# Sliding-window attention and gated convolution on one core: a 32x32-tile convolution for 12 of 56 pairs, and a new order

## The chip, the core and the metric

The kernel runs on one core of a Trainium2 chip. The metric is the device time of one execution in microseconds (us). The profile is one further execution, recorded by the hardware profiler; its times are us, unless ns is written. The engines are PE (matrix multiply; PEld is its weight load), DVE (vector), ACT (scalar, activations), POOL (gpsimd) and SP, which issues the DMA transfers. Every engine works through its own instructions strictly in program order and meets the others at semaphores.

## The reference

```python
scores = 1/sqrt(64) * q @ k.T                     # q, k, v: 8 batches, 8 heads, 576, 64
scores = where(|i - j| <= 32, scores, -1e9)
attn   = softmax(scores);  x = attn @ v           # x: 8, 576, 512
h      = relu(x @ w_in)                           # w_in: 512, 1024
conv   = sum over k of conv_w[k] * h shifted by k - 1   # 3 taps along the sequence, one weight a channel
out    = (h * sigmoid(conv)) @ w_out              # w_out: 1024, 512; out is float32
```

Inputs and output are float32; the kernel multiplies in bf16 and accumulates in float32.

## The kernel before

**An order written out.** The program is a list of some 860 words, ORDER (L30), each a step with its arguments. A loop at L742 calls the step's function. The class Pinned (L183) keeps every instruction in the order in which it was issued on its engine, so ORDER fixes each engine's sequence; since all instructions go through its line 189, nearly every row of the profile has L189, and groups are told apart by the names of tiles. A word such as `sc,0,1,0,m@0+2` is step sc for batch 0, head group 1, half 0, kind m, in PSUM banks 0 and 2. There are eight banks, one tile PS of 8 x 512 floats a partition.

**Attention, a batch b at a time in two groups G of four heads.** lq and lk (L213) load q and k into one of six st buffers, cq and ck (L238) cast them to bf16 on POOL, ACT or DVE, tq and tk (L247) turn them on DVE by 32x32 blocks. lv (L271) loads five 128-row blocks of v into a single buffer vst, cv (L278) casts one to ve, and vo (L281) makes the copy vo of ve that is moved by 64 rows: two 64-partition copies on DVE or ACT, or two SBUF to SBUF transfers on SP (kind t). sc (L297) forms scores of 64 queries against 128 keys with 32-row matmuls, four row groups at once; kind m adds the band mask first by eight matmuls against `band`, otherwise a later mk (L349) multiplies by a 0/1 mask on DVE or POOL. ex (L341) is the exponential on ACT, av (L353) multiplies by v (with a column of ones for the sum), nr (L370) divides on DVE and writes xn. x then has to be turned: xp (L395) on PE with a copy xe out of PSUM on ACT or DVE, or xt (L389), a DMA transpose on SP.

**The feed-forward part, a piece P at a time.** The 8 x 576 rows are cut into twelve pieces of 384 columns; the first two are cut again, so pieces 0 to 3 are half wide (192) and pieces 4 to 13 full. The 1024 channels are eight blocks of 128 partitions, m, taken in pairs m2, so there are 14 x 4 = 56 pairs. For each pair: ph (L429) eight matmuls with w_in; re (L443) the relu on ACT into hT; pc (L500) the convolution; th (L551) a tanh on ACT (the sigmoid is half of 1 + tanh); ga (L572) the gate (1 + tanh) * h on DVE into gT. Then py (L599) multiplies gT with w_out in eight matmuls a 128-row block, ye (L610) copies y out of PSUM (ACT or DVE), st stores it from SP. gT has three buffers, hT three, y four.

**The kinds of convolution.** A weight a channel is a diagonal matrix; three taps are three accumulated matmuls, with the diagonal matrices in diag_w (built by dg, L643).
- P: whole 128x128 matmuls, six a pair. One tanh, one gate.
- A, D: 64x64 matmuls on the four quadrants. The second block of the pair goes through the off-diagonal quadrants, so its halves come out exchanged. A puts them back in three tanh calls, D in three gates.
- S: as A, but two transfers (sw, L568) put the halves back.
- X: no matmul. ACT multiplies the first tap, DVE adds the other two (tp, L540, four instructions a pair).
- Y: two taps on PE, the third on DVE.

A letter z behind the kind means that the tanh goes to an SBUF buffer z, so that the PSUM bank is free earlier; otherwise it stays in PSUM.

**Number of pairs of each kind.** Before: P 14, A 18, D 6, S 2, X 14, Y 2. Of these, full wide: P 3, A 16, D 5, S 2, X 14.

**Start.** s0 to s10 set constants; cw (L639) turns the 3 x 1024 conv weights with one matmul against an identity into conv_w_sb; li, ci and lo, co load and cast w_in and w_out through borrowed buffers.

Of the kernel before, what the change touches and what calls it, by code (L numbers as in the profile page):

```python
# [40 lines left out]
lq,2,1 cv,1,0,a ph,2,2@1 ga,0,3,P ex,1,1,0,1 vo,1,0,d pc,1,3,Pz@4 re,2,3 ex,1,1,0,0 ph,2,1@5 lv,1,4 co,0,d re,2,2
av,1,0,0@6 th,1,3,Pz sc,1,1,1,m@0+2 mk,1,1,0,d re,2,1 pc,2,2,Pz@4 lv,1,3 ck,2,0,a ga,1,3,Pz nr,1,0,0 pc,1,1,Pz@5
th,2,2,Pz tk,2,0 th,1,1,Pz lq,3,0 co,3,p av,1,1,0@6 pc,2,3,P@4 ex,1,1,1,0 pc,1,0,P@5 ex,1,1,1,1 nr,1,1,0 ph,2,0@0
th,2,3,P lk,3,1 cq,2,0,p s6 th,1,0,P ga,1,1,Pz xp,1,0@6 xp,1,1@7 re,2,0 xe,1,0,a sc,1,0,1,m@0+2 lv,2,1 ga,2,3,P
xe,1,1,a pc,2,1,Y@6 ga,1,0,P co,2,a ph,3,3@4 ga,2,2,Pz lq,3,1 co,1,p tq,2,0 pc,2,0,Y@5 ex,1,0,1,1 ph,3,1@7 ex,1,0,1,0
tp,2,1,Y ph,3,2@2 re,3,3 lv,2,0 ck,2,1,p re,3,1 tp,2,0,Y py,0,2@4 th,2,1,Y re,3,2 ga,2,1,Y th,2,0,Y tk,2,1 lk,3,0
cq,2,1,p pc,3,3,Az@6 lk,4,0 pc,3,1,Dz@0 ye,0,2,a ga,2,0,Y cv,1,4,p py,0,1@2 th,3,1,Dz tq,2,1 th,3,3,Az lv,2,2 cv,1,3,p
ga,3,1,Dz vo,1,1,a sc,2,0,0,m@4+0 py,0,0@3 lv,2,3 cq,3,0,p ye,0,1,d ga,3,3,Az ex,2,0,0,1 lq,4,1 av,1,1,1@6 tq,3,0
ck,3,1,a py,1,0@2 st,0,1 cv,2,1,p nr,1,1,1 ex,2,0,0,0 ye,0,0,a av,1,0,1@0 tk,3,1 ye,1,0,a sc,2,0,1,d@4+6 st,0,0
cq,3,1,p ph,3,0@3 ex,2,0,1,0 nr,1,0,1 lv,2,4 pc,3,2,Pz@2 ex,2,0,1,1 re,3,0 sc,2,1,0,d@4+6 tq,3,1 th,3,2,Pz xp,1,2@0  # L50
st,1,0 ck,3,0,p xp,1,3@1 ex,2,1,0,0 xp,1,4@2 ex,2,1,0,1 pc,3,0,Pz@3 xe,1,3,d xe,1,2,a sc,2,1,1,m@4+6 mk,2,1,0,d
xe,1,4,a lk,4,1 tk,3,0 th,3,0,Pz ph,4,0@0 ex,2,1,1,1 lq,4,0 cv,2,2,p ga,3,2,Pz cv,2,0,a ex,2,1,1,0 ph,4,1@2 lv,3,0
ga,3,0,Pz ck,4,0,a mk,2,0,1,d py,1,2@4 re,4,0 tk,4,0 lv,3,2 cq,4,1,p re,4,1 lq,5,0 cv,2,3,a pc,4,0,A@0 tq,4,1 vo,2,0,t
ye,1,2,a ph,4,3@2 th,4,0,A cv,2,4,d lv,3,3 vo,2,1,d pc,4,1,P@4 lv,3,4 re,4,3 ga,4,0,A av,2,0,1@6 th,4,1,P pc,4,3,Az@2
st,0,2 ck,4,1,p nr,2,0,1 ph,4,2@0 th,4,3,Az ga,4,1,P lk,5,0 cq,4,0,p py,1,1@6 tk,4,1 re,4,2 lv,3,1 cv,3,0,p tq,4,0
pc,4,2,Pz@4 lk,5,1 cv,3,2,a ye,1,1,a ga,4,3,Az av,2,1,1@0 th,4,2,Pz sc,3,0,1,d@2+6 st,1,1 cq,5,0,p nr,2,1,1 ex,3,0,1,1
lv,4,0 av,2,1,0@4 ex,3,0,1,0 ga,4,2,Pz xp,2,4@0 xp,2,2@1 xe,2,4,a sc,3,1,1,m@2+6 xt,2,3 cv,3,3,p nr,2,1,0 py,2,0@0
ex,3,1,1,0 xe,2,2,d cv,3,4,a lv,4,2 mk,3,0,1,d ex,3,1,1,1 st,1,2 av,2,0,0@4 vo,3,1,d py,2,1@1 ye,2,0,a lv,4,3 ck,5,0,p
nr,2,0,0 lv,4,4 cv,3,1,a xp,2,0@0 ye,2,1,a xp,2,1@2 vo,3,0,d sc,3,0,0,d@4+6 xe,2,0,a py,2,2@3 xe,2,1,a tq,5,0 lk,6,1
ck,5,1,p ex,3,0,0,0 lk,6,0 ex,3,0,0,1 tk,5,0 sc,4,1,1,m@4+0 lv,4,1 cv,4,0,p ye,2,2,a av,3,1,1@6 mk,3,0,0,d lq,6,0  # L60
ph,5,0@2 ex,4,1,1,0 nr,3,1,1 ex,4,1,1,1 lq,5,1 cv,4,2,p av,3,0,1@4 re,5,0 st,2,1 sc,3,1,0,m@0+6 nr,3,0,1 pc,5,0,Pz@2
ex,3,1,0,0 lv,5,0 cv,4,3,p ex,3,1,0,1 tk,5,1 xt,3,2 cv,4,4,p sc,4,0,1,d@0+4 th,5,0,Pz ph,5,3@6 vo,4,1,d ex,4,0,1,0
ex,4,0,1,1 xt,3,3 ga,5,0,Pz ph,5,1@0 re,5,3 mk,4,0,1,d ck,6,1,a av,3,1,0@2 lv,5,3 av,3,0,0@4 nr,3,1,0 ph,5,2@6 re,5,1
st,2,0 nr,3,0,0 ck,6,0,a pc,5,1,Dz@0 cv,4,1,d xp,3,0@2 re,5,2 xp,3,1@3 lk,7,1 cq,6,0,p av,4,0,1@4 xe,3,0,a xe,3,1,d
xp,3,4@6 pc,5,2,Xz nr,4,0,1 ph,6,3@2 vo,4,0,t cq,5,1,p xe,3,4,a tp,5,2,Xz th,5,1,Dz ph,6,1@4 lq,7,1 re,6,3 cv,5,0,p
lv,5,2 lq,6,1 sc,4,0,0,d@0+6 ph,6,0@2 re,6,1 lv,6,0 ex,4,0,0,1 ex,4,0,0,0 ph,6,2@4 ga,5,1,Dz lv,5,1 cv,5,3,p re,6,0
st,2,2 th,5,2,Xz pc,5,3,Az@6 re,6,2 ph,7,0@0 lv,6,3 mk,4,0,0,d th,5,3,Az ga,5,2,Xz pc,6,0,Az@2 lv,5,4 ph,7,1@4 tq,5,1
re,7,0 th,6,0,Az lk,7,0 pc,6,2,D@0 ga,5,3,Az ph,7,2@6 tk,6,0 lq,7,0 cv,5,2,p re,7,1 pc,6,1,A@2 th,6,2,D ga,6,0,Az
py,3,0@4 re,7,2 lv,6,2 cq,6,1,p ga,6,2,D th,6,1,A pc,6,3,Az@6 py,3,1@5 ye,3,0,d th,6,3,Az ga,6,1,A st,3,0 pc,7,0,Dz@0
tq,6,0 ye,3,1,a sc,4,1,0,m@2+6 th,7,0,Dz cv,5,4,p py,3,2@4 st,3,1 ga,6,3,Az ex,4,1,0,1 vo,5,1,t ex,4,1,0,0 tq,6,1  # L70
ck,7,0,p sc,5,0,1,m@6+0 lv,6,4 ye,3,2,a av,4,1,1@2 tk,6,1 ex,5,0,1,0 cq,7,1,p st,3,2 ph,7,3@4 ex,5,0,1,1 nr,4,1,1
cq,7,0,p pc,7,1,Az@0 re,7,3 av,4,1,0@6 ck,7,1,d xt,4,3 av,4,0,0@2 th,7,1,Az py,4,1@4 cv,6,3,p nr,4,1,0 xt,4,2 cv,6,0,a
cv,5,1,d sc,5,1,1,m@0+6 nr,4,0,0 cv,6,4,p ye,4,1,a vo,5,0,t py,4,2@5 ex,5,1,1,1 ga,7,1,Az ex,5,1,1,0 xt,4,1 ga,7,0,Dz
av,5,1,1@6 ye,4,2,a xp,4,0@4 lv,6,1 sc,5,1,0,p@0+2 xe,4,0,a py,4,0@5 xt,4,4 nr,5,1,1 ex,5,1,0,0 ex,5,1,0,1 lv,7,0
tk,7,1 mk,5,1,0,p pc,7,2,Az@6 st,4,1 av,5,0,1@0 lv,7,3 th,7,2,Az ye,4,0,d pc,7,3,Az@2 st,4,2 tq,7,1 ph,8,2@4 st,4,0
cv,6,1,p th,7,3,Az lv,7,4 nr,5,0,1 ph,8,0@6 lv,7,1 ga,7,2,Az xt,5,4 re,8,2 sc,5,0,0,m@0+2 re,8,0 ga,7,3,Az ph,8,1@4
# [28 lines left out]
def kernel(  # L105
# [98 lines left out]
    def unit(b, G):  # L204
        return 2 * b + G
# [574 lines left out]
```

## Time and profile before

| | us |
|---|---|
| median of 3 runs (217.8 to 219.38) | 219.03 |
| the profiled execution | 217.15 |
| its span, first to last instruction | 215.4 |
| DMA transfers, GB/s over the span | 221 |
| PE busy: matmuls with w_in / with w_out / convolution | 70.9 / 65.5 / 27.9 |
| DVE busy: tap products of X / gates out of z | 31.1 / 45.3 |
| ACT busy: relu / exponential / tanh out of PSUM into z | 40.2 / 39.0 / 33.6 |
| POOL busy: casts of q and k / of v | 32.2 / 15.4 |

Busy is the time in which at least one instruction of the group runs. Matmuls overlap one another, so a busy PE isn't a PE at its peak; what a step costs there is read from the start of one group to the start of the next. In the chain of waits each piece is the work that was waited for at that time, followed back from the end of the program.

### The profile page before, as it was taken

How to read it: one execution, taken by the hardware profiler on the slowest of the kernel's cores; microseconds unless marked ns; L12 is line 12 of the kernel's file. 1: busy time of each engine (PE TensorE's matmuls, PEld its weight loads, DVE VectorE, ACT ScalarE, POOL GpSimd, SP SyncE). 2: the span in 40 equal slices, each digit the busy share in tenths (PEclk: the TensorE clock that was granted, in tenths of full speed). 3: DMA queues.
4: the chain of work that ended last, by engine and by line, in shares of the span. 5: the costliest groups of instructions: out<-in, count | busy, mean ns of one | idle time of the engine just before them, and what ended most of it. 6: DMA issues, size and time to landing. Idle time of an engine off the chain costs nothing.

```text
span 215.4 us, 7416 instructions
## 1 busy us (share of the span) xinstructions
PE 194.5 (90%) x3113; PEld 116.0 (54%) x3134; DVE 186.9 (87%) x303; ACT 181.4 (84%) x318; POOL 62.5 (29%) x69
## 2 busy tenths in 40 slices
PE   2076998999999879999999999999999999999994
PEld 1055997855755546655445556455553554545443
DVE  5977499989999998998989898989899889999920
ACT  6686599899998767999977779999889898999951
POOL 5636754565323753340336050100300000000000
PEclk9999999999999999999999999999999999999999
DMA  6999999999999999999986569676236205311143
GB/s 222 315 245 394 382 287 401 332 326 337 315 375 264 324 193 348 288 242 306 262 284 186 128 158 246 138 194 185 102 94 109 97 27 158 95 34 49 53 190 146
DMA packets 63253, 47.58 MB, mean 221 GB/s; under 512 B 50012, under 2 KB 52596, under 8 KB 63220
## 3 DMA queue, kind: packets, MB, share of 16 engines
q1 hardware_dynamic: 63184, 47.10, 75.4%
q8 instruction: 24, 0.39, 0.8%
q14 instruction: 9, 0.07, 0.1%
q10 hardware_dynamic: 36, 0.01, 0.1%
HBM read 32.52 MB, written 9.44 MB: 195 GB/s over the span
## 4 chain that ended last, share of the span: by engine, by line
PE 63%; DVE 18%; ACT 5%; SPq 5%; issue 4%; DMA 4%; DVEq 0%
PE PS L189 63%; SPq L189 5%; DVE gT L189 3%; DVE qT L189 3%; DVE xn L189 3%; DVE kT L189 3%; DVE vo L189 3%; DMA vst<-in_v_dram 2%; DMA out_dram<-y 2%; ACT attn L189 2%; DVE attn L189 1%; ACT hT L189 1%; DVE rec L189 1%; ACT xT L189 1%; DVE xT L189 1%
## 5 line engine op out<-in xcount | busy, mean ns | idle before, releaser
L189 PE MATMUL PS<-xT,w_in_sb 128*128 128x385 bf16 (+3 forms) x448 | 70.9, 309 | 0.5 <-ACT z L189 0.4
L189 PE MATMUL PS<-w_out_sb,gT 128*128 128x512 bf16 (+1 forms) x275 | 65.5, 374 | 1.7 <-issue 0.9
L189 PEld LDWEIGHTS <-w_in_sb 128*128 128x128 bf16 x448 | 41.3, 100 | 22.4 <-issue 2.3
L189 DVE SCALAR_TENSOR_TENSOR gT<-z,hT 128x768 bf16<-128x768 f32 (+4 forms) x55 | 45.3, 838 | 5.2 <-ACT z L189 3.8
L189 ACT ACTIVATE hT<-PS 128x770 bf16<-128x770 f32 (+3 forms) x56 | 40.2, 731 | 6.8 <-PE PS L189 6.4
L189 PEld LDWEIGHTS <-gT 128*128 128x128 bf16 x296 | 26.9, 98 | 30.7 <-issue 2.8
L189 ACT ACTIVATE attn<-PS 128x512 bf16<-128x512 f32 (+1 forms) x64 | 39.0, 657 | 3.1 <-PE PS L189 2.7
L189 POOL TENSOR_SCALAR qb<-st 128x1152 bf16<-128x1152 f32 x25 | 32.2, 1288 | 30.7 <-DMA st<-in_q_dram 13.1
L189 ACT ACTIVATE z<-PS 64x384 f32<-64x384 f32 (+4 forms) x66 | 33.6, 512 | 4.4 <-PE PS L189 3.4
L189 DVE SCALAR_TENSOR_TENSOR z<-hT,conv_w_sb,z 128x384 f32<-128x384 bf16 x56 | 31.1, 618 | 0.6 <-ACT z L189 0.6
L189 PE MATMUL PS<-hT,diag_w 64*64 64x384 bf16 (+3 forms) x404 | 27.9, 307 | 0.0
L189 DVE TENSOR_TENSOR xn<-PS,rec 128x512 bf16<-128x512 f32 (+1 forms) x32 | 26.4, 824 | 1.1
L189 ACT COPY y<-PS 128x512 f32<-128x512 f32 (+1 forms) x30 | 17.3, 581 | 9.8 <-PE PS L189 8.9
L189 POOL TENSOR_SCALAR ve<-vst 128x512 bf16<-128x512 f32 x23 | 15.4, 676 | 33.3 <-DMA vst<-in_v_dram 26.0
L189 PE MATMUL PS<-qT,kT 32*128 32x64 bf16 x1152 | 15.7, 195 | 5.3 <-DVE qT L189 5.1
L189 DVE STREAM_TRANSPOSE qT<-qb 128x576 uint32<-128x576 uint32 x16 | 19.9, 1244 | 0.5 <-POOL qb L189 0.3
L189 DVE STREAM_TRANSPOSE kT<-qb 128x576 uint32<-128x576 uint32 x16 | 19.9, 1244 | 0.4 <-ACT qb L189 0.4
L189 PEld LDWEIGHTS <-diag_w 64*64 64x64 bf16 (+1 forms) x404 | 14.5, 104 | 10.4 <-issue 6.8
L189 PEld LDWEIGHTS <-kT 32*128 32x128 bf16 x1152 | 13.5, 96 | 10.8 <-issue 5.1
L189 PEld LDWEIGHTS <-attn 128*64 128x64 bf16 x640 | 13.3, 117 | 9.5 <-issue 6.3
L189 PE MATMUL PS<-ve,attn 128*64 128x65 bf16 x384 | 16.0, 203 | 2.4 <-ACT attn L189 1.4
L189 ACT ACTIVATE z<-hT,conv_w_sb 128x384 f32<-128x384 bf16 x28 | 15.7, 610 | 0.2
(53 smaller groups left out, 158.6 us busy)
## 6 DMA issues: line engine op xcount, KB each, us to landing
st<-in_k_dram SPq DMA_DIRECT2D x16, 576.0 KB, 6.3
st<-in_q_dram SPq DMA_DIRECT2D x16, 576.0 KB, 7.6
out_dram<-y SPq DMA_DIRECT2D x35, 256.0 KB, 2.8
vst<-in_v_dram SPq DMA_DIRECT2D x24, 256.0 KB, 6.1
vst<-in_v_dram SPq DMA_DIRECT2D x16, 192.0 KB, 5.8
vo<-ve SPq DMA_DIRECT2D x16, 130.0 KB, 2.4
xT<-in_moe_w_in_dram SPq DMA_DIRECT2D x2, 512.0 KB, 6.3
xT<-in_moe_w_out_dram SPq DMA_DIRECT2D x2, 512.0 KB, 7.0
```

Of the source, the lines that this page charges most:

```text
L189: return lambda *args, **kwargs: tc.keep_in_program_order(do(*args, **kwargs))
```

## The change

- A new kind Q for 12 pairs (six quads of four neighbouring blocks, in pieces 6, 7, 9, 11 and 13): step pq multiplies with 32x32 diagonal matrices on all sixteen tiles of the array. Block i of the quad sends its row strip r to the column strip (r + i) mod 4. So that the result comes out in place, blocks 1 to 3 are first rotated by 32, 64 and 96 partitions: step rt copies them from hT to a new buffer hR (two of them) by six SBUF to SBUF transfers on SP, after the relus of both pairs.
- The kinds are chosen anew: P 13, A 8, D 3, X 20, Q 12. Full wide: P 1, A 7, D 3, X 17, Q 12. S, sw and Y are gone. P now uses 64x64 matmuls on the two diagonal quadrants, twelve a pair.
- The conv weights are turned in three parts: cw and cwx for the straight 64x64 matrices, and cx0, cx and cxx (four matmuls at shifted columns) for the rotated 32x32 ones. diag_w becomes two tiles with 64 and 32 columns, built by dg and dh.
- Small constants share the y buffers; the buffer z of a pair is the one of its m2; unused code for a late form of q and k is gone.
- ORDER is planned anew, with other engines for many steps:

| step | before | after |
|---|---|---|
| vo: DVE / ACT / transfer | 6 / 2 / 8 | 15 / 0 / 1 |
| mask: by matmul / DVE / POOL | 15 / 15 / 2 | 22 / 5 / 5 |
| x turned: PE and copy / DMA transpose | 18 / 22 | 10 / 30 |
| cast of v: POOL / ACT / DVE | 23 / 10 / 7 | 34 / 4 / 2 |
| cast of q and k: POOL / ACT / DVE | 25 / 6 / 1 | 28 / 3 / 1 |
| y out of PSUM: ACT / DVE | 30 / 7 | 31 / 6 |

```diff
+    hR_ = tiles(2, [128, 3, CH + 4], BF16, "hR")
-    diag_w = tiles(1, [128, MB, 3, 128], BF16, "diag_w")[0]
+    diag_w = [pp.tile([128, MB // 4, 4, 3, x], BF16, name=f"diag_w{x}") for x in (32, 64)]
...
+    def rt(P, q):
+        c, half = pieces[P]
+        kind = c % 3
+        n = CH + (4 if kind == 1 else 2)
+        h = hT_[kind].rearrange("p (q i) x -> p q i x", i=4)
+        for i in range(1, 4):
+            for p0, p1, a in ((0, 128 - 32 * i, 32 * i), (128 - 32 * i, 128, 0)):
+                sync.dma_start(hR_[q][p0:p1, i - 1, 0:n], h[a:a + p1 - p0, q, i, 0:n])
...
+    def tap(ps, P, m, kk, n, lo, to, h=None, i=0):
+        tensor.matmul(
+            ps[to:to + n], diag_w[n // 64][lo:lo + n, m // 4, m % 4, kk, :],
+            taps(P, m if h is None else i, kk, (lo, n), h), start=(kk == 0), stop=(kk == 2),
+        )
...
+        elif kind[0] == "P":
+            for i, m in enumerate(ms):
+                for kk in range(3):
+                    for lo in (0, 64):
+                        tap(ps[:, i, :], P, m, kk, 64, lo, lo)
...
+    def pq(P, q, kind, banks):
+        w = width(P)
+        for kk in range(3):
+            for i in range(4):
+                for r in range(4):
+                    tap(
+                        PS[:, banks[i // 2] + i % 2, 0:w], P, 4 * q + i, kk, 32, 32 * r, 32 * ((r + i) % 4),
+                        hR_[q] if i else None, i - 1,
+                    )
...
-    def sw(P, m2):
-        for lo in (0, 64):
-            sync.dma_start(where["z", P, m2][lo:lo + 64, 1, :], where["zs", P, m2][64 - lo:128 - lo, :])
...
+    def cx(bank):
+        where["cx"] = PS[:, bank, 0:3 * MB]
+        for i in range(4):
+            tensor.matmul(
+                PS[:, bank, 3 * MB * i:3 * MB * i + 3 * MB], conv_w24[:, 32 * i:32 * i + 128], ident24,
+                start=True, stop=True,
+            )
+
+    def dh(q, e):
+        to = diag_w[0][:, q].rearrange("p i k x -> p (i k) x")
+        {"d": vector, "p": gpsimd}[e].tensor_tensor(
+            out=to, in0=eye32[:, None, :].broadcast_to([128, 12, 32]),
+            in1=conv_w_sb[0][:, q].rearrange("p i k -> p (i k)")[:, :, None].broadcast_to([128, 12, 32]),
+            op=ALU.mult,
+        )
```

The pq steps and their rt in the new order, with what stands between on PE in one case:

```
... re,6,2 ... rt,6,1 ph,6,0@0 av,4,0,1@4 av,4,0,0@2 ph,7,2@6 ... ph,7,0@4 ... ph,7,1@2 sc,5,1,1,p@0+6 ... py,3,1@4 pq,6,1,Qz@2+6 py,3,2@5 th,6,3,Qz th,6,2,Qz ...
```

More of the change, by code (lines that the diff above doesn't have):

```diff
@@ L96 @@
[L96 to L100 removed]
+lk,0,0 s0,d s5 s1 s2 s9 ck,0,0,a lq,0,0 lq,0,1 lv,0,1 lk,0,1 lv,0,0 lv,0,2 lv,0,4 s1d cw@1 s11 s3,p cwx s4 s7 dg,4,d
@@ L167 @@
     unit_ = band[:, 256:384].rearrange("p (e x) -> p e x", e=2)
-    band2 = tiles(1, [128, 192], BF16, "band2_")[0]
-    mask1 = tiles(1, [128, 64], BF16, "mask1_")[0]
-    conv_w24 = tiles(1, [3 * MB, 128], FP32, "conv_w24")[0]
+    once = y_[NY - 2]
+    mask1, eye32 = once[:, 0:32].bitcast(BF16), once[:, 32:48].bitcast(BF16)
+    eye64 = once[:, 128:160].bitcast(BF16)
+    conv_w_sb = [
+        t.rearrange("p (q i k) -> p q i k", i=4, k=3)
+        for t in (once[:, 48:48 + 3 * MB], tiles(1, [128, 3 * MB], FP32, "conv_w_sb")[0])
+    ]
+    conv_w24, ident24 = y_[NY - 1][0:3 * MB, 0:256], y_[NY - 1][0:3 * MB, 256:256 + 3 * MB]
     PS = pq.tile([128, 8, 512], FP32, name="PS")
@@ L300, in sc @@
         ts = tiles_of(h)
-        if b >= LATE:
-            qx, kx = late(0, b), late(1, b)
-            for a in range(4 if on == "m" else 0):
-                p = slice(64 * (a % 2), 64 * (a % 2) + 64)
-                tensor.matmul(
-                    PS[:, banks[a // 2] + a % 2, 0:64 * len(ts)], band2[p, 0:128],
-                    band2[p, None, 128:192].broadcast_to([64, len(ts), 64]), start=True, stop=False,
-                )
-            for i, t in enumerate(ts):
-                for a in range(4):
-                    p = slice(64 * (a % 2), 64 * (a % 2) + 64)
-                    tensor.matmul(
-                        PS[:, banks[a // 2] + a % 2, 64 * i:64 * i + 64],
-                        kx[p, 2 * G + a // 2, 64 * t:64 * t + 128], qx[p, 2 * G + a // 2, 64 * t:64 * t + 64],
-                        start=(on != "m"), stop=(on != "m" or t == ts[-1]),
-                    )
-            return
         if on == "m":
@@ L465, in re, with taps @@
         scalar.activation(to, ps, AF.Relu, bias=0.0, scale=0.5)
-    def taps(P, m, kk, part=None):
+    def taps(P, m, kk, part=None, h=None):
         c, half = pieces[P]
@@ L471, in taps @@
         step = HW + (2 if kind == 1 else 0)
-        hT = hT_[kind] if part is None else hT_[kind][part:part + 64]
+        hT = hT_[kind] if h is None else h
+        hT = hT if part is None else hT[part[0]:part[0] + part[1]]
         ms = slice(m, m + 1) if isinstance(m, int) else slice(m[0], m[1] + 1)
@@ L533, in pc, with tap_w @@
                     for lo in (0, 64):
-                        to = 64 - lo if i else lo
-                        tensor.matmul(
-                            ps[to:to + 64, i, :], diag_w[lo:lo + 64, m, kk, lo:lo + 64],
-                            taps(P, m, kk, lo), start=(kk == 0), stop=(kk == 2),
-                        )
+                        tap(ps[:, i, :], P, m, kk, 64, lo, 64 - lo if i else lo)
+    def pq(P, q, kind, banks):
+        w = width(P)
+        for kk in range(3):
[5 more added lines that the diff above has]
+                    )
+        for y in range(2):
+            m2 = 2 * q + y
+            where["pc", P, m2] = psum2(banks[y], w, True)
+            if kind[1:] == "z":
+                z_of(P, m2)
+    def tap_w(m, kk):
+        return conv_w_sb[1][:, m // 4, m % 4, kk:kk + 1]
     def tp(P, m2, kind):
-        ps = where["pc", P, m2]
-        for kk in ((1,) if kind[0] == "Y" else (1, 2)):
+        for kk in (1, 2):
             for i in range(2):
                 m = 2 * m2 + i
-                o = like(ps[:, i, :], P)
+                o = like(where["pc", P, m2][:, i, :], P)
                 vector.scalar_tensor_tensor(
-                    out=o, in0=taps(P, m, kk), scalar=conv_w_sb[:, kk, m:m + 1], in1=o,
-                    op0=ALU.mult, op1=ALU.add,
+                    out=o, in0=taps(P, m, kk), scalar=tap_w(m, kk), in1=o, op0=ALU.mult, op1=ALU.add
                 )
@@ L556, in tanh @@
             scalar.activation(out_, in_, AF.Tanh, bias=0.0, scale=1.0)
-        if kind[0] == "S":
-            tanh(where["z0s", P, m2], ps)
-            return
         if kind[0] != "A":
@@ L639, in cw @@
     def cw(bank):
-        tensor.matmul(PS[:, bank, 0:3 * MB], conv_w24, ident24, start=True, stop=True)
-        vector.tensor_copy(out=conv_w_sb.rearrange("p k m -> p (k m)"), in_=PS[:, bank, 0:3 * MB])
-    def dg(m, e):
-        if e != "a":
-            {"d": vector, "p": gpsimd}[e].tensor_tensor(
-                out=diag_w[:, m, :, :], in0=ident[:, None, :].broadcast_to([128, 3, 128]),
-                in1=conv_w_sb[:, :, m:m + 1].broadcast_to([128, 3, 128]), op=ALU.mult,
-            )
-        else:
-            for kk in range(3):
-                scalar.activation(
-                    diag_w[:, m, kk, :], ident, AF.Copy, bias=0.0, scale=conv_w_sb[:, kk, m:m + 1]
-                )
+        where["cw"] = ps = PS[:, bank, 0:3 * MB]
@@ new lines, in cw, with cwx, cx0 @@
+        tensor.matmul(ps, conv_w24[:, 0:128], ident24, start=True, stop=True)
+    def cwx():
+        vector.tensor_copy(
+            out=conv_w_sb[1].rearrange("p q i k -> p (q i) k"), in_=where["cw"].rearrange("p (k m) -> p m k", k=3)
+        )
+    def cx0():
+        vector.tensor_copy(out=conv_w24[:, 128:256], in_=conv_w24[:, 0:128])
+    def cx(bank):
[5 more added lines that the diff above has]
+            )
@@ new lines, in cxx @@
+    def cxx():
+        ps = where["cx"]
+        vector.tensor_copy(
+            out=conv_w_sb[0].rearrange("p q i k -> p i q k"),
+            in_=bass.AP(ps.tensor, ps.offset, [list(ps.ap[0]), [3 * MB + 1, 4], [4, MB // 4], [MB, 3]]),
+        )
+    def dg(m, e):
+        to, w = diag_w[1][:, m // 4, m % 4], conv_w_sb[1][:, m // 4, m % 4]
+        if e == "a":
+            for kk in range(3):
+                scalar.activation(to[:, kk, :], eye64, AF.Copy, bias=0.0, scale=w[:, kk:kk + 1])
+            return
+        {"d": vector, "p": gpsimd}[e].tensor_tensor(
+            out=to, in0=eye64[:, None, :].broadcast_to([128, 3, 64]),
+            in1=w[:, :, None].broadcast_to([128, 3, 64]), op=ALU.mult,
+        )
@@ L661, in s1, with s1d, s11 @@
     def s1():
-        scalar.dma_start(conv_w24, moe_conv_w.rearrange("k (m p) -> (k m) p", p=128))
+        scalar.dma_start(conv_w24[:, 0:128], moe_conv_w.rearrange("k (m p) -> (k m) p", p=128))
         make_identity(nc, ident)
+        vector.memset(mask1, 1.0)
+    def s1d():
         vector.tensor_copy(out=ident24, in_=ident[0:3 * MB, 0:3 * MB])
-        vector.memset(mask1, 1.0)
+        for r in range(2):
+            vector.tensor_copy(out=eye64[64 * r:64 * r + 64], in_=ident[64 * r:64 * r + 64, 64 * r:64 * r + 64])
+    def s11():
+        for r in range(4):
+            vector.tensor_copy(out=eye32[32 * r:32 * r + 32], in_=ident[32 * r:32 * r + 32, 32 * r:32 * r + 32])
     def s2():
```

234 lines of the change are left out of this document (91 added, 143 removed).

## The prediction

> **What bounds the kernel now.** I read the busy shares and slices of the page first, then the same busy times by stage, the chain of waits in order of time, the groups of instructions by form, and single stretches of PE, DVE and POOL in order of time.
>
> ```profile
> PE 194.5 (90%) x3113; PEld 116.0 (54%) x3134; DVE 186.9 (87%) x303; ACT 181.4 (84%) x318; POOL 62.5 (29%) x69
> ```
>
> Three engines are nearly full, so taking work from one is worth only what the other two leave.
>
> ```profile
> 0.00:20.00 20.00, 7.51 (x220) 5.80 (x222) 15.23 (x42) 14.92 (x27) 10.45 (x19) 1.00 0.91 284
> 20.00:95.00 75.00, 71.19 (x1370) 49.78 (x1371) 68.18 (x103) 63.34 (x116) 37.21 (x35) 1.00 1.09 319
> 95.00:200.00 105.00, 103.42 (x1451) 54.37 (x1463) 97.51 (x152) 94.79 (x162) 14.87 (x15) 1.00 0.56 151
> 200.00:215.40 15.40, 12.42 (x83) 6.01 (x82) 6.00 (x10) 8.33 (x15) 0.00 (x0) 0.99 0.36 136
> ```
>
> The columns are the stretch, its length, then PE, PEld, DVE, ACT and POOL busy, granted clock, DMA share, GB/s. From 95 us PE is busy 98.5%; POOL has 47.7 of its 62.5 us before 95 us. The clock is 1.00 and plays no part.
>
> ```profile
> 85.86 0.02 issue
> 85.88 0.31 DVE xn L189
> 86.19 0.56 issue
> 86.75 1.25 DVE kT L189
> 88.00 0.03 issue
> 88.03 0.43 DVE vo L189
> 88.46 0.03 issue
> 88.49 1.31 DVE vo L189
> ...
> 94.67 12.97 PE PS L189 x135
> 107.64 0.05 issue
> 107.69 5.09 PE PS L189 x76
> ```
>
> The chain goes through DVE in most of its pieces from 25 to 94 us, and through PE alone from 94.67 us to the end. So PE work is worth its full size late, DVE work early.
>
> ```profile
> 62.81 0.68 PE L189 MATMUL PS<-hT,diag_w 64*64 64x384 bf16 x12
> 63.42 1.49 PE L189 MATMUL PS<-xT,w_in_sb 128*128 128x385 bf16 x8
> 64.75 1.14 PE L189 MATMUL PS<-hT,diag_w 128*128 128x384 bf16 x6
> ...
> 71.94 0.48 PE L189 MATMUL PS<-qT,kT 32*128 32x64 bf16 x40
> ```
>
> From start to start: a crossed pair (A, D, S: twelve 64x64 matmuls, four at once) takes 0.61 us, eight 128x128 ones take 1.33, or 0.166 each.
>
> ```profile
> L189 DVE COPY vo<-ve x12: 424/426/1385, 13.5 to 88.5; 64x1040 bf16<-64x1040 bf16 x12
> ```
>
> ```profile
> 88.03 1.76 DVE L189 COPY vo<-ve 64x1040 bf16<-64x1040 bf16 x2
> ```
>
> The same copy takes 0.42 or 1.39 us. In order of time the long ones are those that begin under a POOL cast (64.78: cast until 65.89; 88.49: cast until 89.5): DVE waits for POOL's instruction to end. The page on SBUF of the Trainium skill, section "Who interferes with whom", says that DVE copies in a two-port mode, and DVE operations with two SBUF inputs, and GpSimd lock each other out for a whole instruction; the trace agrees for these copies.
>
> **The change, part by part, against the profiled execution (217.15 us, span 215.4, 1.75 around it).** That execution is 1.9 below the median of the three runs.
>
> *PE.* Before: 23 crossed full pairs x 0.61 = 14.0; 3 half ones x 0.37 (timeline at 25.3) = 1.1; 3 straight full pairs x 1.0 (six x 0.166) = 3.0; 11 half ones x 0.5 = 5.5; two Y x 0.33 = 0.7; X uses no PE. Sum 24.3. After: 10 x 0.61 = 6.1; 1 x 0.37; 1 x 1.0; 12 x 0.5 = 6.0; six pq steps. A pq has 48 32x32 matmuls of 384 columns. Bounds: three rounds of sixteen at 0.20 a round (0.61 / 3 rounds of four) give 0.61; if only four ran at once, 12 x 0.20 = 2.4. By issue, 40 score matmuls went out in 0.46 us, so 48 in 0.55. Forty-eight also need 48 weight loads, as the scores did, inside those 0.46. I take 0.65, nearest to the crossed row, so 3.9. Sum 17.4: **-6.9**. Masks by matmul go from 15 to 22 score steps at 0.25: +1.7. Transposes by PE go from 18 to 10 at 0.23: -1.8. Four small fp32 matmuls in the start, beside loads. **PE -7.0.**
>
> *The same, by a rule.* The page on TensorEngine Tiling of the Trainium skill, section "Gotcha 1: PSUM Pressure", says that different row tiles cannot use one PSUM bank at the same time. Each of the four blocks of a pq sends four row strips into one bank. By that rule a bank's twelve matmuls go one after another (12 x 0.166 = 2.0 a pq, +8 us in all). The crossed pair speaks against it, since its two row halves share a bank and still finish in 0.61.
>
> *DVE.* X pairs from 14 full to 17 full and 3 half, Y gone: tap products 56 to 68 at 0.555 (31.1/56) and 4 to 12 half ones at 0.40: +9.9. vo: 6 steps to 15, so 12 to 30 copies at 0.426: +7.7 undisturbed. Mask products 15 to 5: 3.9 instead of 11.6: -7.7. Gates: 37 full ones x 0.966, 3 D x 1.78, 16 half about 0.66 = 51.6, against rows that add up to 54.1: -2.5. Casts of v, xT, w_out and y from DVE: -4.9. Turned weights and memsets to smaller tiles or POOL: -1.6; eight new small copies +1.0. **+1.9.**
> Then the lock. I compared each DVE row with the median of its form in order of time: 16 instructions lost 8.3 us together. Some 89 DVE instructions of the exposed kind (vo, cv, masks, products and gates out of SBUF) stand ahead of POOL's last cast in the old order, 144 in the new one; so 0.094 us each, times a POOL share that rises by about a tenth, gives 14.9: **+6.6**. Bounds: 0 (the new order keeps them apart) to +12 (masks on POOL hold 2.13 us a piece, row of the two that are there). I take the middle, the same loss per exposed instruction. **DVE 195.4.**
>
> *ACT.* Taps of X +5.3; tanh -6.2 (a crossed full pair takes three, 1.47, a Q pair one, 0.82); casts of xT -3.4, v -3.8, q/k -3.6; vo -4.2; turned weights -2.8; w_in +2.1; y +0.6. **-16.**
>
> *POOL.* v casts 23 to 34 (+7.4), q/k 25 to 28 (+3.9), masks 2 to 5 (+6.4 to 8.5), turned weights +3, rest about 0. **+21, about 84.** It has room; what it costs is DVE's wait, counted above. Cover gone, its casts would hold the transposes of q and k.
>
> *SP and DMA.* Rotated copies: six rt steps of six transfers, issue 0.574 (vo row) to 0.626 (z row) each: 3.5 us a step, +21 in all. DMA transposes 22 to 30 at 1.26: +10; vo transfers 16 to 2: -8; z swaps -2.5. SP runs ahead of need and has 99 us of waits of its own, mostly for y rows, so I cost this at nothing. The cover: from the later relu of a quad to its pq stand four to six matmul steps of 1.3 to 1.7, 7 to 9 us; a rt needs 3.5 issue and 2.3 to 2.4 landing (z and vo rows), 5.9. Thin: 1 to 3 us. Behind an rt that waits for its relu stand loads of q, k, v and stores; the readers are POOL's casts and the y buffers. Cover gone: 2 to 3 us each, 12 to 18.
>
> *Start and end.* The first loads and casts change order, with three of four first q/k casts on POOL or ACT as before; -1 to +2, I take 0. The last pieces end in the same py, ye and store: 0.
>
> *Sum.* If PE stayed the bound, -7. But DVE has 195.4 - 15.2 (first 20 us) - 6.0 (last 15.4) = 174.2 for the middle, where it had 165.7 in 180. In 40 to 100 us, where it carries the chain, it is busy 56.5 of 60, 94%. 174.2 / 0.94 = 185.3: +5.3. ACT's relief takes away about half of DVE's 5.4 us of waits for ACT: -2.7. Span 215.4 + 2.6 = 218.0, execution 219.8; moved by 1.9 to stand with the median, 221.7, so **222** against 219.03.
>
> **Rivals.**
> *PE stays the bound, faster.* POOL and DVE are kept apart (loss stays 8.3, DVE 188.8) and DVE idles 4% in the middle: 167.6 / 0.96 = 174.6, span 210.0, with the 1.75 and 1.9 **214**. For it: from 180 to 200 us DVE is busy 19.77 of 20, so a tight order exists; ACT's 16 us less loosen every hand-over. Against it: that stretch has no POOL work. It decides when DVE's extra work and loss stay under about 4 us.
> *No change.* The loss grows by half as much (+3.3): 174.2 - 3.3 = 170.9 / 0.94 = 181.8, +1.8 less 2.7: **218**.
> *Rotated copies late.* Two or three us in most of six places, 12 to 18 less what other engines hide: **227**. For it: SP has waited up to 7.4 us for a y row; against: 7 to 9 us between relu and pq.
> *Banks take one strip at a time.* The four row strips of a block go to one PSUM bank; if they go one by one, twelve matmuls x 0.166 = 2.0 a pq instead of 0.65, +8 on PE; DVE hides about 5 of them: **225**. Against it: the two halves of a crossed pair share a bank and overlap. This is the rule of the TensorEngine Tiling page above.
> *The change does not do what it says:* the Q pairs save nothing, pq at 1.22 (two crossed pairs): +3.4 on PE, hidden under DVE: **222** again.
>
> **How the numbers follow.** Forecast 0.30 (own range 221 to 226); PE stays the bound 0.33 in all its strengths (210 to 216.8); no change 0.25; copies late 0.08; banks 0.04. Forecast, copies and banks make slower, 0.42. The bounds of the lock (0 to +12, at 0.94: -7 to +6 on 222) and of the copies give the range 212 to 229. Within 1% (216.8 to 221.2, about what a measurement of this kernel can tell from no change): 0.25.
>
> **What would show it.** Right: DVE over 192 us and PE under 189, ACT under 168, POOL over 78; vo copies and tap products with maxima above 1.2 us and means above 0.55 and 0.65; the chain through DVE beyond 95 us, well into the stretch where it was PE alone. pq: 48 matmuls start to start in 0.6 to 0.75. Wrong: PE at 98% from about 30 us on; vo at a mean near 0.45; the weight loads or matmuls of a pq waiting for a DMA into hR; a pq over 1.2.

## The result, and the profile after

The changed kernel takes **233.09 us** (median of 4 runs, 231.72 to 234.23), the kernel before 219.2 beside it: ratio 1.0653, 95% interval 1.0565 to 1.0742. It is slower, as forecast, and by more than the range allowed. The profiled execution has a span of 231.6 us, against 215.4. The median of the kernel before moved between 217.5 and 219.2 from one session to the next, so below the ratios are compared, not the medians. A ratio leaves out executions more than 1.5% above the fastest of their kernel, and the mean of the kernel before then lies between 216.3 and 218.7 us by session, so gaps of 1% between the ratios of two sessions are not read.

First the busy times, the clock by slices and the chain of waits of the kernel after:

```profile
PE 200.6 (87%) x3338; PEld 117.8 (51%) x3338; DVE 208.7 (90%) x314; ACT 166.2 (72%) x285; POOL 87.3 (38%) x97
PEclk9999999999999999997999999998599999999999
DVE 44%; PE 29%; SPq 9%; DMA 6%; issue 5%; ACT 4%; POOL 1%; DVEq 0%; ACTq 0%; POOLq 0%
```

ACT fell by 15 us and POOL rose by 25, about as forecast; DVE rose by 22 where 8.5 were forecast. The chain now goes through DVE for 44% of the span and through PE for 29%. The same stretches as before (length, then PE, PEld, DVE, ACT, POOL busy, clock, DMA share, GB/s):

```profile
20.00:95.00 75.00, 66.93 (x1338) 45.35 (x1335) 70.39 (x104) 57.80 (x111) 41.48 (x41) 1.00 0.95 270
95.00:200.00 105.00, 94.53 (x1482) 50.70 (x1480) 99.68 (x135) 78.66 (x130) 35.33 (x28) 0.95 0.76 175
```

From 95 us on PE is idle for 10.5 us where it was idle for 1.6, its clock is down to 0.95, and POOL is busy 35.3 us of 105 where it was 14.9. Now DVE's groups by form (count, busy us, mean ns, idle before) and the copies of vo (min/median/max ns):

```profile
L196 DVE SCALAR_TENSOR_TENSOR z<-hT,conv_w_sb,z 128x384 f32<-128x384 bf16 x68 | 40.4, 660 | 0.2
L196 DVE SCALAR_TENSOR_TENSOR gT<-z,hT 128x768 bf16<-128x768 f32 x35 | 38.9, 1131 | 2.2 <-ACT z L196 1.9
L196 DVE COPY vo<-ve 64x1040 bf16<-64x1040 bf16 x30 | 20.4, 680 | 1.2 <-POOL ve L196 0.5
```

```profile
L196 DVE COPY vo<-ve x30: 424/426/2742, 14.7 to 174.9; 64x1040 bf16<-64x1040 bf16 x30
```

Before, these means were 618, 984 and 675 ns, and 12 copies were made. One such place, DVE and POOL in order of time:

```profile
99.88 3.45 DVE L196 COPY vo<-ve 64x1040 bf16<-64x1040 bf16 x2
```

```profile
99.15 1.15 POOL L196 TENSOR_SCALAR qb<-st 128x1152 bf16<-128x1152 f32 x1
100.27 2.78 POOL L196 TENSOR_TENSOR attn<-attn,mask 128x1280 bf16<-128x1280 bf16 x1
```

The second copy, of 0.43 us where nothing disturbs it, begins under a POOL mask, takes 2.74 us and ends 0.28 us after the mask. I call **loss** what each DVE instruction takes beyond the first quartile of its own form, where that is over 60 ns: 8.4 us in 16 instructions before, **27.9 us in 42** after. DVE's work without it is 178.5 us before and 180.8 after, +2.3. All 42, like the 16 before, begin while a POOL instruction runs and end less than 0.9 us behind it, the ten late copies of vo always 0.28 us after it. Divisions and transposes of q and k (rec, xn, qT, kT) begin under POOL as well in the changed kernel, 42 of them, and none of these is late.

What it does to PE is seen at the longest stall, on DVE, POOL and PE in order of time:

```profile
152.30 4.37 DVE L196 SCALAR_TENSOR_TENSOR gT<-z,hT 128x384 bf16<-128x384 f32 x3
156.78 2.48 DVE L196 COPY vo<-ve 64x1040 bf16<-64x1040 bf16 x2
159.29 1.25 DVE L196 SCALAR_TENSOR_TENSOR gT<-z,hT 128x768 bf16<-128x768 f32 x1
160.46 0.22 DVE L196 RECIPROCAL rec<-PS 128x12 f32<-128x12 f32 x1
160.71 0.96 DVE L196 TENSOR_TENSOR xn<-PS,rec 128x768 bf16<-128x768 f32 x1
```

```profile
152.71 2.13 POOL L196 TENSOR_TENSOR attn<-attn,mask 128x1024 bf16<-128x1024 bf16 x1 [3.14 <-ACT attn L196]
154.81 4.17 POOL L196 TENSOR_SCALAR qb<-st 128x1152 bf16<-128x1152 f32 x3
158.94 2.07 POOL L196 TENSOR_SCALAR ve<-vst 128x512 bf16<-128x512 f32 x2
```

```profile
157.19 0.48 PE L196 MATMUL PS<-qT,kT 32*128 32x64 bf16 x40
161.72 0.51 PE L196 MATMUL PS<-hT,diag_w 32*32 32x384 bf16 x4 [4.06 <-DVE xn L196]
...
162.84 2.76 PE L196 MATMUL PS<-xT,w_in_sb 128*128 128x385 bf16 x8
```

POOL works without a break from 152.7 to 161; DVE is stretched under it; the division of batch 6 that frees a pq's PSUM bank comes late, and PE waits 4.06 us for it; and after the gap eight matmuls take 2.69 us start to start where they took 1.33.

**Where the time went, by PE.** I took every run of like matmuls from its start to the next run's, and called the fastest fifth over seven traces what it needs; the rest is stall or slow clock. (In the trace of before some 20 records of matmuls with w_out are missing; they are put at the others' 68.6 us.)

| us | before | after | short POOL instructions (below) | those and masks by matmul |
|---|---|---|---|---|
| needed | 194.4 | 187.7 | 187.7 | 189.1 |
| stalls and slow clock | 17.1 | 40.8 | 31.5 | 29.8 |
| of it in 20 to 40 us | 2.7 | 8.2 | 7.9 | 6.9 |
| span (with first and last 3 to 4 us) | 215.4 | 231.6 | 222.3 | 222.2 |

The change saves PE 6.7 us of work and adds 23.7 us of standing still.

### The profile page after: what moved, and what is told of

Same layout as the page of the kernel before. It is cut to its first block, busy times and chain, and to the rows that moved or that the text cites. A ratio compares the mean times of both kernels' runs of the same rounds, so it can differ in the third digit from the quotient of the medians.

```text
span 231.6 us, 7860 instructions
## 1 busy us (share of the span) xinstructions
PE 200.6 (87%) x3338; PEld 117.8 (51%) x3338; DVE 208.7 (90%) x314; ACT 166.2 (72%) x285; POOL 87.3 (38%) x97
## 4 chain that ended last, share of the span: by engine, by line
DVE 44%; PE 29%; SPq 9%; DMA 6%; issue 5%; ACT 4%; POOL 1%; DVEq 0%; ACTq 0%; POOLq 0%
PE PS L196 29%; DVE z L196 11%; DVE gT L196 11%; SPq L196 9%; DVE vo L196 6%; DVE xn L196 5%; DVE kT L196 3%; DMA st<-in_q_dram 3%; DMA out_dram<-y 3%; ACT z L196 3%; DVE qT L196 3%; DVE rec L196 1%; DVE attn L196 1%; ACT attn L196 1%; POOL qb L196 1%
## 5 line engine op out<-in xcount | busy, mean ns | idle before, releaser
L196 DVE SCALAR_TENSOR_TENSOR gT<-z,hT 128x768 bf16<-128x768 f32 (+2 forms) x58 | 56.8, 998 | 2.3 <-ACT z L196 1.9
L196 POOL TENSOR_SCALAR qb<-st 128x1152 bf16<-128x1152 f32 x28 | 36.1, 1296 | 38.0 <-DMA st<-in_k_dram 20.5
L196 DVE SCALAR_TENSOR_TENSOR z<-hT,conv_w_sb,z 128x384 f32<-128x384 bf16 (+1 forms) x80 | 46.8, 649 | 0.2
L196 ACT ACTIVATE attn<-PS 128x640 bf16<-128x640 f32 (+1 forms) x64 | 38.9, 656 | 8.8 <-PE PS L196 8.5
L196 PEld LDWEIGHTS <-gT 128*128 128x128 bf16 x296 | 27.1, 98 | 29.8 <-issue 1.4
L196 POOL TENSOR_SCALAR ve<-vst 128x512 bf16<-128x512 f32 x34 | 25.5, 762 | 36.8 <-DMA vst<-in_v_dram 32.9
L196 ACT ACTIVATE z<-PS 128x384 f32<-128x384 f32 (+4 forms) x48 | 27.1, 573 | 10.6 <-PE PS L196 10.3
L196 PE MATMUL PS<-hT,diag_w 64*64 64x192 bf16 (+2 forms) x360 | 21.4, 299 | 5.6 <-DVE xn L196 4.3
L196 ACT ACTIVATE z<-hT,conv_w_sb 128x384 f32<-128x384 bf16 (+1 forms) x40 | 21.3, 584 | 3.0 <-DVE gT L196 2.9
L196 POOL TENSOR_TENSOR attn<-attn,mask 128x1280 bf16<-128x1280 bf16 (+1 forms) x5 | 13.2, 2632 | 23.4 <-ACT attn L196 23.4
L196 DVE COPY vo<-ve 64x1040 bf16<-64x1040 bf16 x30 | 20.4, 680 | 1.2 <-POOL ve L196 0.5
L196 PE MATMUL PS<-vo,attn 128*64 128x65 bf16 x256 | 16.4, 208 | 4.0 <-DVE vo L196 3.9
```

The source lines that it names most:

```text
L196: return lambda *args, **kwargs: tc.keep_in_program_order(do(*args, **kwargs))
```

## The experiments

Theory **Lock**: DVE's loss under POOL's instructions is the cause. Rival **Work**: it is DVE's added work, or PE's waits for other hand-overs, and the loss sits in slack. Rival **Q**: the new convolution itself costs. Later came **Order** (a loss costs only where it falls ahead of a hand-over), **Start** and **Copies**.

### Masks off POOL (e1_mask_matmul)

```diff
-sc,3,1,1,p@2+6 ... mk,3,1,1,p
+sc,3,1,1,m@2+6            (so for all five POOL masks)
```

> The changed kernel, with the five mask products on POOL replaced by masks by matmul (40 more matmuls, about 1.25 us of PE; mathematically the same). Three theories. Lock: DVE waits for POOL's instructions to end, 28 us in the changed kernel against 8 before, and the idle PE and the clock that falls behind it follow from that; the five masks, 2.1 to 2.8 us each, stand behind 8.0 of the 28. It expects DVE's loss near 20, DVE busy near 200, time 222 to 227 (233.1 now). Work: what counts is DVE's added work (tap products and copies), whoever else runs; these masks aren't DVE work, so 232 to 235. Q: the 32x32 kind with its rotated copies and its PSUM banks is what holds things up: 232 to 235.

Ratio 1.0359 (1.0268 to 1.0450); POOL 73.9 us, loss 21.7, span 223.4. Five instructions of POOL less give back 8 of the 16 us of span, although PE does five mask steps more. Lock holds; but the masks' own time on POOL is gone too, so this run alone doesn't tell the lock from masks that come late.

### Short POOL instructions (e6_short_pool)

```diff
-cq,2,1,p
+cq,2,1,0,p cq,2,1,1,p     (casts of q, k and v in halves)
-gpsimd.tensor_tensor(out=attn, in0=attn, in1=mask[:, 0:4 * n], op=ALU.mult)
+for i in range(0, 4 * n, n): gpsimd.tensor_tensor(out=attn[:, i:i + n], in0=attn[:, i:i + n], in1=mask[:, i:i + n], op=ALU.mult)
```

> The changed kernel with the same POOL work cut into shorter instructions: casts of q, k and v on POOL in two halves, mask products on POOL in four quarters. POOL's sum stays (a little more for the starts). Lock expects that DVE waits only to the end of a shorter instruction: loss 28 to about 13 to 17, time 233 down to 220 to 226. Work expects 232 to 235. Order expects the same as Lock if DVE's loss falls, and no change if it doesn't.

Ratio 1.0279 (1.0211 to 1.0347): 3.5% less than the changed kernel, with the same work on every engine, POOL's cut into more pieces. The busy times of this kernel, and its row of vo copies:

```profile
PE 197.1 (89%) x3338; PEld 117.0 (53%) x3338; DVE 202.6 (91%) x314; ACT 165.7 (75%) x285; POOL 112.9 (51%) x174
```

```profile
L197 DVE COPY vo<-ve x30: 424/516/961, 15.4 to 166.1; 64x1040 bf16<-64x1040 bf16 x30
```

POOL is busy 25.6 us more, so DVE meets it more often (71 instructions lose time, not 42), but it waits for a shorter piece: the longest copy is 0.96 us instead of 2.74, the loss 22.3. This is the clearest run for Lock: nothing is changed but how long POOL holds on at a time. A whole mask takes longer here (4 x 1.10 us instead of 2.76), so masks that come late are not what e1 took away. The size isn't settled: Lock expected a loss of 13 to 17, and the span fell by 9.3 us where the loss fell by 5.6. The stretches in which PE's granted clock was 0.50 shrank as well, from 10.2 us to 3.8; that they make up the rest is not shown.

### Both (e7_mask_short)

> Both: masks by matmul instead of POOL (226.1 alone) and POOL's casts in halves. Lock expects the loss of 21.7 to fall to 10 to 13 and the time to 217 to 222. Work 225 to 228.

The edits of both. Ratio 1.0300 (1.0195 to 1.0405): no gain over either alone, and Lock's 217 to 222 is missed. The loss is 11.7 us, DVE's busy time 194.5 (from 95 to 200 us it now has 10.0 us free, with short instructions alone 2.0), and yet the span stays at 222.2. The chain, and the wait that took DVE's place, in this kernel:

```profile
PE 55%; DVE 18%; DMA 14%; SPq 4%; ACT 3%; POOL 2%; issue 2%; DVEq 0%; ACTq 0%; POOLq 0%
```

```profile
119.94 2.98 PE PS L197 x70
122.92 6.87 DMA hR<-hT
```

PE now waits 3.0 us for rotated copies; in the changed kernel it waited for none. So there is a second floor under the lock.

### The same dose in both kernels (e4_before_pool, e13_after_pool)

```diff
 cq,2,1,p
+hold    (54 times: a POOL copy of 128x384 bf16 into a buffer that nobody reads)
```

> The kernel before, with 54 more POOL instructions that copy a constant to an unused tile (384 elements, about 0.4 us each, 22 us in all), one behind each POOL cast of v and two behind each of q or k from batch 2 on; nobody reads the result. DVE, ACT and PE have the same work in the same order. Lock expects DVE's loss to go from 8.4 us to 13 to 17 and the time up by 3 to 8 us (222 to 227 where before is 219). Work and Q expect 0 to 1 us more, from casts that come later.

> The changed kernel with 54 extra POOL copies of 384 elements behind its casts: the same dose that raised the loss of DVE in the kernel before from 8.4 to 13.8 us and its time by 0.7 us. Theory Slack (the kernel before has DVE time to spare while PE carries the chain, the changed one has none): loss up by 5 to 8 us and the time by at least as much, 238 to 243. Rival (POOL's interference costs little in either kernel, and what short instructions gave came from elsewhere): 233 to 235.

Kernel before with it: loss 13.8 us (from 8.4), ratio 1.0045 (0.9996 to 1.0093), under 1%; Lock's 222 to 227 is missed. Changed kernel with it: loss 33.7 (from 27.9), ratio 1.0990 (1.0921 to 1.1058), 3.2% above the changed kernel, some 7 us. The same 54 copies cost 0 to 2 us in the kernel before. The rows by stage, 95 to 200 us, say why: before DVE has 7.5 us free there and PE carries the chain alone; with the dose in the changed kernel,

```profile
95.00:200.00 105.00, 93.41 (x1527) 49.95 (x1526) 102.08 (x133) 77.59 (x128) 56.54 (x56) 0.95 0.68 174
```

DVE is busy 102.1 of 105. A loss costs where DVE has no time left, and there it costs about its whole size (some 7 us for 5.8 us more of loss).

### Masks onto POOL in the kernel before (e5_before_mask_pool), and short instructions there (e9_before_short)

```diff
-mk,3,0,1,d
+mk,3,0,1,p    (five of fifteen; the other run: the cuts of e6)
```

> The kernel before, with five of its DVE mask products (3,0,1; 4,0,1; 4,0,0; 6,1,0; 7,1,0) on POOL: the mirror of the experiment that took five masks from POOL in the changed kernel. DVE has 3.9 us less work. Lock expects each mask to hold DVE by about 1.6 us, as the five of the changed kernel did (8.0 in all): DVE's loss from 8.4 to 14 to 17, and 3 to 7 us more time (222 to 226 where before is 218.5). Work expects no change or 1 us less, 217 to 219. A third theory has come up with the misses of the first four runs, Order: the hand-over of a step's result to the next engine is planned tightly, and any step that ends late is passed on, whatever makes it late; a mask takes 2.1 to 2.8 us on POOL instead of 0.7 to 0.8, so av comes 1.5 to 2 us later in five places: 219 to 224.

> The kernel before with its POOL work cut in the same way. Its loss is 8.4 us; Lock expects 4 to 5, and 1 to 4 us less time (215 to 218 where before is 218.5), not the whole of the loss, since from 95 us on PE carries the chain. Work expects no change.

Five masks on POOL: loss 13.9 us, ratio 1.0048 (0.9996 to 1.0100), so Lock's 222 to 226 is missed too; but DVE's work without the loss also falls, by 4.2 us, so its busy time rises by only 1.3. Short instructions: the loss falls only to 7.7 us, where Lock said 4 to 5, and no change can be told: the ratio of 0.9915 (0.9829 to 1.0001) stands on two of ten executions, and the median of all ten is 218.43 against 218.11. In the kernel before the lock is worth little, as the dose showed.

### Copies of vo from DVE to ACT (e2_vo_act)

```diff
-vo,4,1,d
+vo,4,1,a    (batches 2 to 7, 22 copies)
```

> The changed kernel, with the vo copies of batches 2 to 7 (11 steps, 22 copies) on ACT instead of DVE. Takes 22 x 0.426 = 9.4 us of DVE work and the 7 us that these copies lose under POOL; adds 22 x 1.06 = 23 us to ACT, which would be at 189. Lock and Work both expect less: Work alone (9.4 less) 226 to 229, Lock on top of it (16.4 less) 219 to 225, with DVE busy near 193. Q expects 232 to 235.

Ratio 1.1031 (1.0955 to 1.1107): every theory missed. DVE fell to 192.9 us and its loss to 20.8, but ACT rose to 188.8, and the copies, 1.06 us each there, stood in ACT's order up to four in a row, twice of these just ahead of an exponential (from 103.71 us, for one, 4.26 us of copies). Who waited for whom (total us, times, longest us):

```profile
DVE rec L194 <- PE PS L194: 14.1, 11, 4.1
PE PS L194 <- ACT attn L194: 11.2, 10, 3.8
```

DVE then waited 14.1 us for PE, and PE 11.2 for ACT's exponentials, where it had waited 3.0 in the changed kernel. In a written-out order, work moved to a freer engine delays what stands behind it there.

### Q pairs undone (e3_q_crossed)

```diff
-rt,6,1 ... pq,6,1,Qz@2+6
+pc,6,2,Az@2 pc,6,3,Az@6   (six quads as twelve crossed pairs, no rotated copies)
```

> The changed kernel, with the 12 Q pairs as crossed pairs (kind A) at the same places, and without the six rotation steps (36 transfers). PE gets 6 x (1.22 - 0.75) = 2.8 us more, ACT 12 x 0.65 = 7.8 more; DVE's gates stay as they are. Lock and Work expect 232 to 236: no change or the PE's 2.8 at most. Q expects a gain, 225 or less, because the transfers and the four banks at once are gone.

Ratio 1.0862 (1.0784 to 1.0940), 2% above the changed kernel: the Q pairs, with their rotated copies, save some 4 us. Rival Q falls.

### Two hand-overs moved (e10_handover)

```diff
-tp,5,3,Xz tp,5,0,Xz tp,5,2,Xz tk,5,1 vo,4,1,d ga,5,1,Az vo,4,0,d
+tp,5,3,Xz vo,4,1,d tp,5,0,Xz tp,5,2,Xz tk,5,1 vo,4,0,d ga,5,1,Az
-vo,6,0,d ga,8,0,Xz ph,9,2@2 av,6,0,1@4 nr,6,0,1
+ph,9,2@2 av,6,0,1@4 nr,6,0,1 vo,6,0,d ga,8,0,Xz
```

> The changed kernel with its work and its lengths untouched; only DVE's order is changed at the two places where PE stood still longest: the vo copy of batch 4, second half, goes ahead of two tap products and the gate of 5,1 behind the other vo copy; the division of 6,0,1 goes ahead of a vo copy and a gate. Theory Order (a lock costs only where it falls ahead of a hand-over that PE is waiting for): the two stalls of 3.6 and 4.1 us and the slow clock behind each (1.1 and 1.3) mostly go, 224 to 227 us, while the loss of DVE stays near 28 us. Theory Lock by sum (DVE is full, so its whole loss is added whatever the order): 231 to 234 us.

Ratio 1.0625 (1.0548 to 1.0701): no difference from the changed kernel that can be told. The median, 230.29 us, lies above Order's 224 to 227 and just below the other theory's 231 to 234. The 4 us stall went, and the time came back in small ones (total us, times, longest us):

```profile
PE PS L194 <- DVE xn L194: 7.6, 12, 1.2
```

This wait is 7.6 us as in the changed kernel, now in 12 pieces of at most 1.2 instead of 7 of at most 4.1. From 95 to 200 us DVE is busy 103.4 of 105. So Order falls, in the size it forecast: where DVE is full, its time comes out as stalls on PE, and moving two of them gained little or nothing.

### The start, and all together (e11_start, e12_short_moves_start, e15_w_in_first)

```diff
-pc,0,1,Xz ... tp,0,1,Xz
+pc,0,1,Pz@1               (so for 2,2 and 3,1: twelve tap products fewer)
-li,2 lq,1,0 ... lv,1,1 li,3
+li,2 li,3 lk,1,0 lq,1,0   (e15 alone, with its cast and two ph steps earlier)
```

> The changed kernel with three half pairs of the first pieces (0,1; 2,2; 3,1) convolved by matmuls instead of on ACT and DVE: 12 tap products fewer on DVE (some 6 us before 80 us), 1.9 us more on PE. Theory Start (PE's work done by 40 us is some 5 us behind the kernel before, since DVE carries the chain there): 3 to 5 us faster, 228 to 230. Rival, the start is set by the loads and casts: within 1 us, 232 to 234, or slower by PE's 1.9.

> The changed kernel with all three: POOL's casts in halves and its masks in quarters, the two moves of DVE's order, the three half pairs by matmul. If the three causes are separate, short instructions alone gave 224.2, the moves take at most 3 more (the same two places stand for 1.6 and 1.8 us there) and the start 3 to 5: 216 to 219, about the kernel before or a little faster. If DVE's sum or the loads set the time: 222 to 225.

> The kernel with short POOL instructions (224.2), with the last quarter of w_in loaded and cast ahead of batch 1's q, k and v, as in the kernel before, and two of its matmul steps on PE ahead of the scores of batch 1. Theory Loads (PE falls 5 us behind by 40 us for want of work, since the weights it could work with come late): 220 to 222. Rival (DVE's transpositions carry that stretch and the loads are DMA-bound in either order): 224 to 227.

e11: 1.0845 (1.0768 to 1.0922), no gain over the changed kernel; PE's stalls in 20 to 40 us went from 8.2 only to 6.5, and its work rose by 1.7. e12, which has short instructions, the two moves and the start: 1.0371 (1.0281 to 1.0460), no better than short instructions alone, and 216 to 219 is missed. e15: 1.0426 (1.0380 to 1.0472), no gain over them; 7.6 us of stalls in that stretch. Neither DVE's tap products nor the place of the last quarter of w_in explains why PE stands 5 us more than before between 20 and 40 us. That cause stays open.

### Rotated copies earlier (e14_rt_early)

```diff
-xt,4,3 st,3,0 lq,6,1 lk,6,1 ... rt,7,1
+rt,7,1 xt,4,3 st,3,0 lq,6,1 lk,6,1    (on the kernel of e7)
```

> The kernel with masks by matmul and short casts, whose loss is 11.7 us and which still takes 224.6: there PE waited 3.2 us for the rotated copies of the second Q quad, which stood on SP behind a DMA transpose of 3.9 us. Here that rt step goes ahead of the transpose. Theory Copies (with DVE out of the way the rotated copies are the next wait): 220 to 222. Rival (some other hand-over takes its place, the late transpose among them): 224 to 226.

Ratio 1.0401 (1.0346 to 1.0457), no gain over e7. The wait for hR went from 3.0 to 0.5 us, and this came instead, on PE and on ACT:

```profile
133.40 0.31 PE L197 MATMUL PS<-band 32*128 32x320 bf16 x2 [2.39 <-ACT y L197]
```

```profile
127.70 1.07 ACT L197 COPY y<-PS 128x512 f32<-128x512 f32 x2 [2.82 <-DMA out_dram<-y]
132.76 0.58 ACT L197 COPY y<-PS 128x512 f32<-128x512 f32 x1 [3.25 <-DMA out_dram<-y]
```

The six transfers of rt, the first of which waits for its relu, hold SP for 5.4 us; a transpose of 1.8 us follows, then the stores of y; ACT waits for a y buffer, PE for the bank. Copies alone is not the floor; SP's order is full at that place too.

## Why the prediction was right or wrong

**Right.** *Direction and mechanism*: DVE became the bound, through POOL, and PE's saving was not collected. *PE -7.0*: needed work fell by 6.7. One of the forecast's signs failed all the same: PE's busy time was to fall under 189 and rose from 194.5 to 200.6 (some 3 us of it are the records missing before), so the saving shows only from start to start. *pq at 0.65, bounds 0.61 to 2.4*: 0.75, start to start, in this stretch of PE:

```profile
200.28 0.34 PE L196 MATMUL PS<-hT,diag_w 32*32 32x384 bf16 x4
...
200.68 0.42 PE L196 MATMUL PS<-hR,diag_w 32*32 32x384 bf16 x12
201.03 1.25 PE L196 MATMUL PS<-w_out_sb,gT 128*128 128x512 bf16 x5
```

So "banks take one strip at a time" falls: the rule of the Trainium skill's TensorEngine Tiling (Array Packing), "Gotcha 1: PSUM Pressure", would have made it 2.0, and four row strips into one bank, each to its own 32 partitions of it, overlapped here. "Q pairs save nothing" falls by e3. *ACT -16*: -15.2. *POOL about 84*: 87.3. *DVE's work +1.9*: +2.3.

**Wrong: the term "Then the lock ... +6.6", with its upper bound of +12.** It measured **+19.5** (27.9 against 8.4). The step carried the old loss of 0.094 us per exposed instruction over to the new order, times a POOL share that rises "by about a tenth". Both factors failed. By the forecast's own 84 us, POOL's share of the span rises from 29% to 38%, by a third and not a tenth (that alone would have made the term +9.7). And the share is an average over stages: from 95 to 200 us it went from 14% to 34%, and there 13.6 of the 19.5 us arose (2.0 us of loss before, 15.6 after). The old price, too, came from an order in which the two engines met in 16 of 89 chances; in the new one they met in 42 of 144. A better bound might have been chance itself. If an exposed DVE instruction meets POOL as often as POOL is busy (20 to 200 us), and then waits half of a mean POOL instruction, then (an estimate made afterwards from these rows):

| kernel | exposed x POOL's share x half its mean | estimate, us | measured loss |
|---|---|---|---|
| before | 89 x 0.29 x 0.45 | 11.7 | 8.4 |
| after | 144 x 0.43 x 0.45 | 27.6 | 27.9 |
| masks by matmul (e1) | 144 x 0.35 x 0.40 | 20.0 | 21.7 |
| short instructions (e6) | 144 x 0.56 x 0.32 | 26.2 | 22.3 |
| both (e7) | 144 x 0.43 x 0.29 | 18.2 | 11.7 |
| before with 54 copies (e4) | 89 x 0.47 x 0.38 | 15.9 | 13.8 |
| after with 54 copies (e13) | 144 x 0.62 x 0.41 | 36.7 | 33.7 |

The estimate lies between 8% under and 56% over the measured loss, so how closely it meets the second row is partly luck.

The forecast's own sum, with the measured DVE time in place of 195.4, is (208.7 - 15.2 - 6.0) / 0.94 = 199.5 for the middle, +19.5, less 2.7: a span of 232.2. Measured: 231.6. That it comes so close is in part luck: with the DVE times of e6, e1 and e7 the same sum gives 225.7, 226.0 and 217.1, where the spans are 222.3, 223.4 and 222.2. Nor do the ends of the stated range, 212 and 229, follow from the bounds named for them: -7 and +6 on 222 are 215 and 228.

So the forecast had the cause and got its price wrong. The Trainium skill's page SBUF — State Buffer, "Who interferes with whom", names that cause, an exclusive lock for a whole instruction, and the trace agrees (the copy that ended 0.28 us after the mask).

**Wrong, smaller: "Start and end ... I take 0".** PE stood 4 to 5.5 us longer in 20 to 40 us, in every form of the changed kernel; the bound was +2. Its cause is not found.

**Half right: rotated copies "at nothing".** No matmul waited for hR in the changed kernel; in e7, where DVE was less late, PE waited 3.0 us for it, so the cover was thin, as the text said. Its remark on what stands behind an rt (stores and the y buffers) is what e14 showed.

**Not settled.** With 12 to 22 us of loss the span is 222.2 to 224.5 in four kernels (e6, e7, e14, e15), 7 to 9 above before, though PE needs 5 to 7 us less. The lock accounts for the step from there to 231.6. What holds the span at 222 is not shown: the start, SP's order and perhaps more, each hiding the next. No version that beats the kernel before was found.

## What to carry to other kernels

Price the meeting of DVE and POOL by stage: exposed DVE instructions, times POOL's busy share there, times half of a mean POOL instruction (rough, and made from this one case); it costs its size where DVE is full and almost nothing where another engine carries the chain. If POOL must work beside a full DVE, give it short instructions, even at more busy time. When an engine's saving is not collected, take the covering wait away and look at what is under it before believing that one cause is the whole.

## What the runs showed of the hardware

*Gaps halve PE's clock for a while.* The granted clock was 0.50 from 160.3 to 167.1 us, starting inside the 4.06 us gap that ended at 161.72; eight matmuls with w_in took 2.69 us there instead of 1.33, so that stall of 4 us cost over 5. It was 0.50 from 105.7 to 109.1 us too, starting inside a gap of 2.44 us that ended at 106.40, behind one of 0.67 that ended at 103.38; the sixteen matmuls from 106.93, partly within it, took 3.80 us instead of 2.66. The Trainium skill's TensorE: Matmul & The Clock Gate, Part 1, has the clock fall to half after an idle window of about 3.4 us. The two stretches, of 3.4 and 6.8 us, agree with that length, once and twice; but PE had been idle without a break for only 1.7 and 2.6 us when they began, so here the clock fell sooner. *Cutting POOL's work is dear for POOL*: 28 casts of q and k took 36.1 us, 56 halves 44.7; a mask of 2.76 us took 4 x 1.10. *The lock works both ways*: the copy of 128x384 took POOL at least 504 ns in both kernels, but a median of 511 ns in the kernel before, with DVE partly free, and 682 in the changed one, where DVE is full. Of the 54 long ones (over 560 ns) in the two runs, 51 begin under a gate, tap product, mask or copy of vo on DVE.
